# A Fourier transform and two layers on one core: where the row of column D/2 joins z, and where the first two z are made ready

## The chip, the cores and the metric

The kernel runs on one core of a Trainium2 chip, in one launch. The metric is device time in microseconds of that launch. Five engines work side by side: TensorE (PE, with its weight loads as PEld), VectorE (DVE), ScalarE (ACT), GpSimd (POOL) and SyncE (SP), which here does nothing but issue DMAs, one after the other.

## The reference

```
X = fft(fft(x, axis=1), axis=2).real          # x: 8 x 3072 x 256, float32
x1 = X.reshape(24576, 256)
h = x1 @ w_in;  g = h - tanh(h);  x2 = g @ w_out          # 256 -> 2048 -> 256
h2 = x2 @ w_in2                                            # 256 -> 1024
e = exp(h2 - max(h2));  u = h2 * e / (sum(e) + 1e-9)
out = (u - mean(u)) / sqrt(var(u) + 1e-6) * g_ln @ w_out2  # 1024 -> 256
```

## The kernel before

**The transform** (about the first 168 us) goes over 24 pieces q, three for each of 8 batches. For each piece DVE adds and subtracts rows of x (lines 489, 494, 498), PE multiplies by tables (lines 522, 537, 548), and after a batch's third piece ACT copies the sums out of PSUM (lines 586, 592, 600) and they go to DRAM as z: `z1_d[b]` and `z2_d[b]`, each of the form [2, 128, ...]. The partition is a column d from 0 to 127; the first index u says whether column d was added to its mirror column 256 - d or the mirror was subtracted. For d = 0 the difference is not wanted; in its place, row 0 of u = 1, stands the transform of column D/2 = 128, which `transform_nu` makes for all batches together at q = 3 and writes to `n1_d` and `n2_d`. The same stretch also turns the float64 weights into float32 parts (`narrow`, lines 213 to 223).

**The main loop** has 768 steps: 48 groups n of 256 pairs of output rows (6 for each batch), and 16 blocks m of 128 columns of `w_in` in each. A pass is the 16 steps of one group, with j the step in it. In each step PE makes two sums of a block (`parity` and `even`, line 915), DVE mixes them (`lead`, line 933, and `act_in`, line 940), ACT takes the tanh (line 948), DVE subtracts (line 957), ACT rounds and POOL or DVE makes the remainder (lines 178 and 181), and PE multiplies by `w_out` (line 977). In steps with m = 1, 5, 9 and 13 the remainder is DVE's. Pieces of the second layer are laid between by `layer2`: products (line 1006), minimum and exponential (lines 1028, 1047), and the transposition of u through DRAM: DVE transposes 32 x 32 blocks (line 1085), SP stores them to `mv_d` (line 1087) and reads them back in four DMAs to `um` (line 1091).

**How a z comes in.** A group's z passes one buffer `zf` (bufs=1). In the pass before its own, and at the end of the pass ahead of that, it goes so:

- j = 14: `load_z(n + 2)` issues two DMAs from z1_d or z2_d (line 265), when the z before has left the buffer
- j = 0: `load_row(n + 1)` issues one more DMA, of 2.0 to 3.1 KB, from n1_d or n2_d to row 0 of u = 1 of the buffer (line 271)
- j = 2 and j = 10: DVE takes the first and the second sum over it (`mix_z`, lines 287 and 288)
- j = 3: `load_nu(n + 1)` (line 276) brings `nb`, which the next pass uses
- j = 10 and 11: POOL takes two more sums (line 299), ACT rounds to `zs`, POOL makes the remainder

For n = 0 and n = 1 the same is done in the transform at given q, with all four sums and the remainder on DVE; what is put into `later[q]` is woven into the DVE work that stands ahead of piece q, which is that of piece q + 2.

Each engine takes its instructions in the order in which the program lists them, and so does SP with its DMAs: nothing but that order and the waits sets when something runs.

Of the kernel before, what the change touches and what calls it, by code (L numbers as in the profile page):

```python
# [24 lines left out]
NSJ = NS // P  # L25
HP = P // 2
NQB = HP + 2
THIRD = (P, P, P, 2 * NQB, 2 * NQB, 2 * NQB)
# [8 lines left out]
GPB = PAIRS // GP  # L37
# [112 lines left out]
def fft2_moe_moe_kernel(  # L150
    ctx: ExitStack, tc: tile.TileContext, xr, x8, xn, xn8, w_in, w_out, w_in2, w_out2, g_ln, tt, t8, ft, out
):
    nc = tc.nc
# [12 lines left out]
    n1_d = dram.tile([B, 6 * P], F32, name="n1_d")  # L166
    n2_d = dram.tile([B, 2 * ZW], F32, name="n2_d")
    z1_d = [dram.tile([2, P, 6 * P], F32, name=f"z1_d{b}") for b in range(B)]
    z2_d = [dram.tile([2, P, 2 * ZW], F32, name=f"z2_d{b}") for b in range(B)]
# [7 lines left out]
    def rnd(o, i):  # L177
        nc.scalar.activation(out=o, in_=i, func=AF.Copy)  # L178
# [78 lines left out]
    zg, zc = {}, {}  # L257
# [6 lines left out]
        for u in range(2):  # L264
            nc.sync.dma_start(out=zf[:, u, :, :to], in_=src[u].rearrange("p (w n) -> p w n", w=2)[:, :, :to])

    def load_row(n):
        b, g = divmod(n, GPB)
        src = (n1_d if g < NSJ else n2_d)[b : b + 1]
        to = THIRD[g] * (3 if g % 3 else 2)  # L270
        nc.sync.dma_start(out=zc[n][0:1, 1, :, :to], in_=src.rearrange("o (w n) -> o w n", w=2)[:, :, :to])

    def load_nu(n):
        b, g = divmod(n, GPB)
# [28 lines left out]
    def ready_z(n):  # L303
        yield from mix_z(n, nc.vector)
        yield from sums_z(n, nc.vector)
# [250 lines left out]
    def out_tile(name):  # L556
        return hlp.tile([P, 2 * ZW + 2], F32, tag="zt", bufs=5, name=name)
# [23 lines left out]
    def evict(b):  # L581

        for u in range(2):
            zt = out_tile(f"zt{b}_1_{u}")[:, : 6 * P]
            for w, p in enumerate(acc.pop((1, u))):
                nc.scalar.copy(out=zt[:, w * 3 * P : (w + 1) * 3 * P], in_=p[:, : 3 * P])
            nc.sync.dma_start(out=z1_d[b][u], in_=zt)
        for u in range(2):
            zt = out_tile(f"zt{b}_2_{u}")[:, : 2 * ZW]
            if u == 0:  # L590
                for w, p in enumerate(acc[2, u]):
                    nc.scalar.copy(out=z1536[:, 2 * w : 2 * w + 2, b], in_=p[:, NQB : 3 * NQB + 1 : 2 * NQB])
                if b == B - 1:
                    nc.gpsimd.tensor_tensor(
                        out=z1536[:, 4:6], in0=z1536[:, 0:2], in1=z1536[:, 2:4], op=ALU.subtract
                    )
                    for _ in range(2):
                        nc.gpsimd.tensor_tensor(out=z1536[:, 4], in0=z1536[:, 4], in1=z1536[:, 5], op=ALU.add)
            for w, p in enumerate(acc.pop((2, u))):
                nc.scalar.copy(out=zt[:, w * ZW : (w + 1) * ZW], in_=p[:, :ZW])  # L600
            if u == 0 and b == B - 1:
                rnd(zh[:, 0], z1536[:, 4])
                rest(nc.gpsimd, zh[:, 1], z1536[:, 4], zh[:, 0])
            (nc.scalar if b < B - 1 else nc.sync).dma_start(out=z2_d[b][u], in_=zt)
# [117 lines left out]
    def low(o, i, hi):  # L722
        yield rest(nc.vector, o, i, hi)
# [24 lines left out]
    ready, later = [], {}  # L748
    for q in range(NQ):
        b, j = divmod(q, NSJ)  # L750
        ending = now[:]
        now.clear()
        works = []
        if ahead <= q + 2 < NQ:
            works.append(prep(q + 2))
        works += ready + later.pop(q, [])
        weave(*works)
        weave(*ending)
        ready = coming_weights(q + 1)
        if folds and j == 0:  # L760
            later.setdefault(q + 2, []).append(fold_w_in(*folds.pop()))
        if q == 3:
            transform_nu()
        transform(q)
        if j == NSJ - 1 and q < NQ - 1:
            evict(b)
        for n in range(2):
            if q == 13 + 4 * n:
                load_z(n)
                load_nu(n)  # L770
            if q == 14 + 4 * n:
                load_row(n)
                later.setdefault(q + 1, []).append(ready_z(n))
            if q == 15 + 4 * n:
                whole, hi, lo = by_half(n)
                rnd(hi, whole)
                later.setdefault(q + 2, []).append(low(lo, whole, hi))
        if q == NQ - 4:
            nc.sync.dma_start(out=wnu, in_=wnu_d.rearrange("o (m p) -> p (o m)", p=P))
            nc.sync.dma_start(  # L780
                out=nu_h, in_=nu_d[:, PAIRS : PAIRS + 1].rearrange("b o -> o b").to_broadcast([P, B])
            )
# [49 lines left out]
    def split_wi2(eng, b):  # L832
        split_halves(eng, wi2[:, b, 0], wi2[:, b, 1], whole_of(b))
# [9 lines left out]
    def load_wo2(half):  # L843
        w = wk.tile([P, FF2], F32, tag="u", bufs=3, name=f"wo2r_{half}").rearrange("p (k n) -> p k n", k=4)
        nc.sync.dma_start(out=w, in_=wo2_d[half])
        wg.append((w, wk.tile([P, 4, D], F32, tag="ut", bufs=2, name=f"wg{half}")))
# [358 lines left out]
    for step in range(steps + 3):  # L1205
        n, j = divmod(step, NM)
        if step in at_ab:
            special(at_ab[step])
        if 0 < step <= steps:
            parity(*divmod(step - 1, NM), 1)  # L1210
        if step < steps:
            even(n, j)
        if 0 < step <= steps:
            act_in(*divmod(step - 1, NM))
        if step < steps:
            lead(n, j)
        lag = 3 if step < NM else 2
        for s in range(out_done, min(step - lag + 1, steps)):
            act_out(*divmod(s, NM))
        out_done = max(out_done, min(step - lag + 1, steps))  # L1220
        if step - 1 in wo2_at:
            split_wo2(wo2_at.index(step - 1), True)
        layer2(step, "ahead")
        if 1 < n < NG and j == 3:
            sum_x2(S1)
            sum_x2(S2)
        layer2(step, "early")
        if NM <= step < steps + 2:
            low_by_vector(*divmod(step - 2, NM))
        if step in at_o1:  # L1230
            special(at_o1[step])
        if step in (NM - 1, NM):
            mean_wo2(step - NM + 1)
        if step == NM + 2:
            nc.tensor.matmul(bank_b, wi2[:, B11, 0, :P], wi2[:, B11, 0], start=True, stop=True)
        s1 = step - 5 if step < NM else step - 3
        for s in (range(o1_done, min(s1 + 1, steps))):
            o1(*divmod(s, NM))
        o1_done = max(o1_done, min(s1 + 1, steps))
        layer2(step, "late")  # L1240
        if 0 < n < NG and j in (3, 4):
            for b in ((S3,), (S4,))[j - 3] if n > 1 else ((S1, S2), (S3, S4))[j - 3]:
                sum_x2(b)
        if step in wo1_at:
            c, part = divmod(wo1_at.index(step), 2)
            split_wo1(c + 2, wo1_raw[c + 2], slice(part * 2, part * 2 + 2))
        if step == NM:
            raw1.close()
            mv = pool(mv_stack, "mv", 2, side="right")
        if step in wi2_splits:  # L1250
            split_wi2(nc.gpsimd, wi2_splits[step])
        if step in (2, 3):
            load_wo2(step - 2)
        if 7 <= step < NM - 1:
            gain_wo2(step - 7)
        if step in (NM + 1, NM + 2):
            center_wo2(step - NM - 1)
        if step in wo2_at:
            split_wo2(wo2_at.index(step), False)
        if step == NM + 12:  # L1260
            nc.scalar.copy(out=pas, in_=pa)
        if step == NM + 6:
            special_nu()
        if step == NM + 15:
            special_out()
        if n == NG - 1 and j == 9:

            b12 = zp.tile([P, HF], F32, tag="zf", bufs=1, name="b12")
            nc.sync.dma_start(out=b12, in_=b12_d)
        if n == NG - 1 and j == 12:  # L1270
            split_halves(nc.gpsimd, wt[0][:, 0, 0], wt[0][:, 1, 0], b12)
        if step == NM + 30:
            make_identity(nc, ident)
        if n + 2 < NG and j == 14:
            load_z(n + 2)
        if 1 <= n and n + 1 < NG:
            if j == 0:
                load_row(n + 1)
            if j == 3:
                load_nu(n + 1)  # L1280
            if j == 2:
                mixing = mix_z(n + 1, nc.vector)
            if j in (2, 10):
                next(mixing)
            if j == 10:
                weave(sums_z(n + 1, nc.gpsimd))
            if j == 11:
                whole, hi, lo = by_half(n + 1)
                rnd(hi, whole)
                rest(nc.gpsimd, lo, whole, hi)  # L1290
# [159 lines left out]
```

## Time and profile before

| | |
|---|---|
| median of 3 runs | 2876.41 us (2859.62 to 2878.13) |
| profiled execution | 2867.5 us, of which span 2865.7 us |
| mean granted clock of TensorE | 0.979 of full speed |
| busy: PE, DVE, ACT, POOL | 2701.8, 2312.7, 2039.9, 1981.8 us |
| transform, 0 to 168 us | PE busy 144.15 us, DMA share 0.90 |
| main loop, 168 to 2800 us | PE busy 2496.24 of 2632 us, DMA share 0.43 |

A row of the timeline reads: start and duration in microseconds, engine, line, operation, output<-input, shapes, how many were merged, and in brackets how long the engine had been idle before and what ended that. The duration of merged rows runs from the first start to the last end.

### The profile page before, as it was taken

How to read it: one execution, taken by the hardware profiler on the slowest of the kernel's cores; microseconds unless marked ns; L12 is line 12 of the kernel's file. 1: busy time of each engine (PE TensorE's matmuls, PEld its weight loads, DVE VectorE, ACT ScalarE, POOL GpSimd, SP SyncE). 2: the span in 40 equal slices, each digit the busy share in tenths (PEclk: the TensorE clock that was granted, in tenths of full speed). 3: DMA queues.
4: the chain of work that ended last, by engine and by line, in shares of the span. 5: the costliest groups of instructions: out<-in, count | busy, mean ns of one | idle time of the engine just before them, and what ended most of it. 6: DMA issues, size and time to landing. Idle time of an engine off the chain costs nothing.

```text
span 2865.7 us, 48018 instructions
## 1 busy us (share of the span) xinstructions
PE 2701.8 (94%) x15327; PEld 2394.2 (84%) x15327; DVE 2312.7 (81%) x4830; ACT 2039.9 (71%) x3941; POOL 1981.8 (69%) x1806
## 2 busy tenths in 40 slices
PE   9888999999999999999999999999999999999999
PEld 7677888888888888888888888888888888888888
DVE  8766888788887888788777888788887788888886
ACT  4466777777777777777677777777776777777776
POOL 0057777777777777677677777777776777777774
PEclk9989999999999999999999999999999999999999
DMA  9942444444445344444444444444435344444532
GB/s 364 356 126 54 99 112 97 103 94 109 102 96 113 96 99 111 91 106 98 106 95 97 106 99 93 96 111 98 104 86 114 88 104 97 106 105 93 117 87 67
DMA packets 878307, 322.04 MB, mean 112 GB/s; under 512 B 788640, under 2 KB 836320, under 8 KB 874760
## 3 DMA queue, kind: packets, MB, share of 16 engines
q1 hardware_dynamic: 875736, 313.25, 44.6%
q10 hardware_dynamic: 2016, 5.68, 0.5%
q8 instruction: 122, 2.00, 0.3%
q14 instruction: 129, 1.06, 0.1%
q0 software_dynamic: 304, 0.06, 0.0%
HBM read 180.97 MB, written 137.93 MB: 111 GB/s over the span
## 4 chain that ended last, share of the span: by engine, by line
PE 67%; DVE 11%; DMA 9%; SPq 4%; issue 3%; ACT 3%; POOL 2%; DVEq 0%; ACTq 0%; POOLq 0%
PE x2p L977 27%; PE h L915 14%; PE po L1111 9%; PE bank_a L1006 7%; PE bank_b L1006 5%; DMA zf<-n_d 4%; PE po L1118 4%; SPq L1091 4%; DMA mv_d<-tb 3%; DVE h L940 1%; DVE t L957 1%; DVE gh L181 1%; DVE u L1028 1%; DVE h L957 1%; DVE tb L1085 1%
## 5 line engine op out<-in xcount | busy, mean ns | idle before, releaser
L977 PE MATMUL x2p<-gh,wo 128*128 128x512 f32 x4608 | 1155.9, 387 | 3.7 <-POOL gh L181 3.3
L181 POOL TENSOR_TENSOR gh<-t,gh 128x512 fp32r<-128x512 f32 x584 | 892.2, 1528 | 376.2 <-ACT gh L178 184.9
L977 PEld LDWEIGHTS x2p<-gh,wo 128*128 128x128 f32 x4608 | 843.7, 193 | 131.3 <-POOL gh L181 21.1
L915 PEld LDWEIGHTS h<-zs,wt 128*128 128x128 f32 x4572 | 640.6, 193 | 199.3 <-DVE asb L933 82.5
L948 ACT ACTIVATE t<-h 128x512 f32<-128x512 f32 x762 | 453.4, 595 | 484.0 <-DVE h L940 389.2
L915 PE MATMUL h<-zs,wt 128*128 128x256 f32 x4572 | 665.7, 280 | 128.6 <-DVE gh L181 64.1
L940 DVE SCALAR_TENSOR_TENSOR h<-asb,h 128x256 f32<-128x256 f32 x762 | 323.8, 425 | 274.3 <-PE h L915 271.4
L1111 PE MATMUL po<-wo,ut 128*128 128x512 f32 x1528 | 522.0, 383 | 0.0
L181 POOL TENSOR_TENSOR ut<-um,ut 128x512 fp32r<-128x512 f32 x372 | 477.6, 1284 | 17.8 <-ACT ut L178 14.1
L178 ACT ACTIVATE gh<-t 128x512 fp32r<-128x512 f32 x584 | 369.1, 632 | 162.8 <-DVE t L957 159.4
L181 POOL TENSOR_TENSOR xs<-xb,xs 128x256 fp32r<-128x256 f32 (+1 forms) x282 | 234.4, 831 | 277.6 <-ACT xs L178 154.6
L1118 PE MATMUL po<-wo,ut 128*128 128x256 f32 x1528 | 416.5, 273 | 0.0
L957 DVE TENSOR_TENSOR t<-h,t 128x512 f32<-128x512 f32 x578 | 394.6, 683 | 0.0
L933 DVE SCALAR_TENSOR_TENSOR asb<-nb,wnu,h 128x256 f32<-128x256 f32 x762 | 362.3, 475 | 21.5 <-PE h L915 21.4
L1006 PE MATMUL bank_a<-wi,xs 128*128 128x512 f32 x1128 | 319.3, 393 | 2.5 <-ACT bank_b L1154 1.4
L1111 PEld LDWEIGHTS po<-wo,ut 128*128 128x128 f32 x1528 | 290.2, 190 | 30.3
L1056 DVE SCALAR_TENSOR_TENSOR u<-u,e 128x1024 f32<-128x1024 f32 x188 | 300.9, 1600 | 0.0
L1118 PEld LDWEIGHTS po<-wo,ut 128*128 128x128 f32 x1528 | 293.5, 192 | 0.1
L1006 PEld LDWEIGHTS bank_a<-wi,xs 128*128 128x128 f32 x1128 | 213.0, 195 | 39.0 <-ACT bank_b L1154 8.9
L1006 PE MATMUL bank_b<-wi,xs 128*128 128x512 f32 x846 | 229.8, 380 | 1.8 <-POOL xs L181 1.1
L178 ACT ACTIVATE ut<-um 128x512 fp32r<-128x512 f32 x372 | 229.7, 617 | 1.4 <-PE po L1118 0.7
L1085 DVE STREAM_TRANSPOSE tb<-u 128x1024 f32<-128x1024 f32 x186 | 229.4, 1233 | 0.0
(164 smaller groups left out, 3136.6 us busy)
## 6 DMA issues: line engine op xcount, KB each, us to landing
mv_d<-tb SPq DMA_DIRECT2D x186, 512.0 KB, 2.6
um<-mv_d SPq DMA_DIRECT2D x744, 128.0 KB, 3.7
out<-o SPq DMA_DIRECT2D x192, 128.0 KB, 2.0
x<-xr SPq DMA_DIRECT2D x23, 1024.0 KB, 10.8
zf<-z_d SPq DMA_DIRECT2D x32, 396.0 KB, 4.5
zf<-z_d SPq DMA_DIRECT2D x32, 384.0 KB, 4.7
wi<-w_in SPq DMA_DIRECT2D x6, 1024.0 KB, 9.0
z_d<-zt SPq DMA_DIRECT2D x16, 384.0 KB, 8.7
```

The source lines that it names most:

```text
L178: nc.scalar.activation(out=o, in_=i, func=AF.Copy)
L181: eng.tensor_tensor(out=o, in0=i, in1=hi.bitcast(F32), op=ALU.subtract)
L915: nc.tensor.matmul(in_pairs(hs[n, m][:, 0]), wt[c][:, hw, u, o : o + P], in_turn(zs[:, hz, u]), start=(u == 0 and i == 0), stop=(i == 2), ...
L933: nc.vector.scalar_tensor_tensor(out=asb, in0=zg[n][0], scalar=wnu[:, m : m + 1], in1=hs[n, m][:, 0], op0=ALU.mult, op1=ALU.add)
L940: nc.vector.scalar_tensor_tensor(out=h[:, 1], in0=as_.pop((n, m)), scalar=2.0, in1=h[:, 0], op0=ALU.mult, op1=ALU.subtract)
L948: nc.scalar.activation(out=t, in_=h, func=AF.Tanh)
L957: nc.vector.tensor_tensor(out=g, in0=h, in1=t, op=ALU.subtract)
L977: nc.tensor.matmul(in_pairs(x2p[n][mt]), wo1[c][:, hw, k, mt * P : (mt + 1) * P], in_turn(gh[:, hg]), start=(m == 0 and i == 0), stop=(m = ...
L1006: nc.tensor.matmul(in_pairs(bank), xs[:, hx, xs_at[a]], in_turn(wi2[:, b, hw]), start=(start and q == 0), stop=(q == 2), skip_group_check= ...
L1056: nc.vector.scalar_tensor_tensor(out=u, in0=u if h is None else h, scalar=-1.0 if h is None else 1.0, in1=e, op0=ALU.mult, op1=ALU.mult, a ...
L1111: nc.tensor.matmul(in_pairs(po), ut[:, 0, ks], wo2[:, k].rearrange("p h x n -> p (x n) h"), start=(k == 0), stop=False,)
L1118: nc.tensor.matmul(in_pairs(po[:, :D]), ut[:, 1, ks], wo2[:, k, :, 0].rearrange("p h n -> p n h"), start=False, stop=(k == NK2 - 1),)
```

## The change

`load_row` goes, and with it one small DMA into SBUF for each of 48 groups. `put_rows(b)` comes: two DMAs from DRAM to DRAM, which put batch b's rows from n1_d and n2_d to row 0 of u = 1 of z1_d[b] and z2_d[b]. It is called at q = 7, 10, ... 22 for batches 0 to 5 and at steps 8 and 9 of the main loop for batches 6 and 7. The loads of z then bring the row along. For n = 0 the load moves from q = 13 to q = 10, the four sums from 15 to 13, the rounding from 15 to 14, the remainder from 17 to 15; for n = 1 the load from 17 to 16, the rounding from 19 to 20, while the sums stay at 19 and the remainder at 21. (Line numbers behind line 271 are two lower after the change.)

```diff
-    def load_row(n):
-        b, g = divmod(n, GPB)
-        src = (n1_d if g < NSJ else n2_d)[b : b + 1]
-        to = THIRD[g] * (3 if g % 3 else 2)
-        nc.sync.dma_start(out=zc[n][0:1, 1, :, :to], in_=src.rearrange("o (w n) -> o w n", w=2)[:, :, :to])
+    def put_rows(b):
+        for z_d, n_d in ((z1_d, n1_d), (z2_d, n2_d)):
+            nc.sync.dma_start(out=z_d[b][1, 0:1], in_=n_d[b : b + 1])
...
         if j == NSJ - 1 and q < NQ - 1:
             evict(b)
+        if j == 1 and b > 1:
+            put_rows(b - 2)
         for n in range(2):
-            if q == 13 + 4 * n:
+            if q == 10 + 6 * n:
                 load_z(n)
                 load_nu(n)
-            if q == 14 + 4 * n:
-                load_row(n)
-                later.setdefault(q + 1, []).append(ready_z(n))
-            if q == 15 + 4 * n:
+                later.setdefault(q + 3, []).append(ready_z(n))
+            if q == 14 + 6 * n:
                 whole, hi, lo = by_half(n)
                 rnd(hi, whole)
-                later.setdefault(q + 2, []).append(low(lo, whole, hi))
+                later.setdefault(q + 1, []).append(low(lo, whole, hi))
...
         if step in (2, 3):
             load_wo2(step - 2)
+        if step in (8, 9):
+            put_rows(step - 2)
...
         if 1 <= n and n + 1 < NG:
-            if j == 0:
-                load_row(n + 1)
             if j == 3:
                 load_nu(n + 1)
```

SP in the main loop, from the load of one z to the `nb` that follows it, before:

```order
L265 DMA zf_2183<-z_d_77 128x2x264 [waits DMAHW7_49,Pool_49]
L265 DMA zf_2183<-z_d_77 128x2x264
L1087 DMA mv_d_85<-tb_2239 128x1024 [waits DMAHW0_49,DVE_49]
L1091 DMA um_2242<-mv_d_85 32x32x32 [waits DMAHW0_49]
L1091 DMA um_2242<-mv_d_85 32x32x32 [waits DMAHW2_49]
L1091 DMA um_2242<-mv_d_85 32x32x32 [waits DMAHW3_49]
L1091 DMA um_2242<-mv_d_85 32x32x32 [waits DMAHW4_49]
L271 DMA zf_2183<-n_d 1x2x264 [waits DMAHW7_49,DMAHW5_49]
L276 DMA nb_2352<-nu_d 128x256 [waits DMAHW6_49]
```

and with the change:

```order
L265 DMA zf_2196<-z_d_77 128x2x264 [waits DMAHW4_49,DMAHW3_49,Pool_49]
L265 DMA zf_2196<-z_d_77 128x2x264
L1085 DMA mv_d_85<-tb_2252 128x1024 [waits DMAHW5_49,DVE_49]
L1089 DMA um_2255<-mv_d_85 32x32x32 [waits DMAHW5_49]
L1089 DMA um_2255<-mv_d_85 32x32x32 [waits DMAHW7_49]
L1089 DMA um_2255<-mv_d_85 32x32x32 [waits DMAHW0_49]
L1089 DMA um_2255<-mv_d_85 32x32x32 [waits DMAHW1_49]
L274 DMA nb_2364<-nu_d 128x256 [waits DMAHW2_49]
```

The row's DMA behind the four of `um` is gone, and nothing stands in its place. A DMA's first wait is most often that for the semaphore (DMAHW0 to 7, used in turn) that it is to take; Pool and DVE are waits for engines.

DVE in the transform around the four sums of z 0 (zf_841), before, in the work ahead of piece q = 15:

```order
L489 TENSOR_TENSOR sm_2_910<-x_2_770 128x1024 [waits DMAHW5_49]
L287 TENSOR_TENSOR zf_841<-zf_841 128x4x128 [waits DMAHW2_49,DMAHW1_49,DMAHW0_49]
L494 TENSOR_TENSOR pm_2_911<-sm_2_910 128x512 [waits DVE_49,PE_49]
L494 TENSOR_TENSOR pm_2_911<-sm_2_910 128x512
L288 TENSOR_TENSOR zf_841<-zf_841 128x4x128 [waits DVE_49]
```

and with the change the same place, where the remainder of z 0 (zs_715) now stands; its sums are 18 rows further ahead:

```order
L487 TENSOR_TENSOR sm_2_920<-x_2_780 128x1024 [waits DMAHW4_49]
L181 TENSOR_TENSOR zs_715<-zf_710,zs_715 128x512 [waits Activation_49]
L492 TENSOR_TENSOR pm_2_921<-sm_2_920 128x512 [waits DVE_49,PE_49]
L492 TENSOR_TENSOR pm_2_921<-sm_2_920 128x512
L496 TENSOR_TENSOR pm_2_921<-pm_2_921 128x256 [waits DVE_49] x2
```

DVE waits there for ACT instead of DMAs. ACT's rounding of z 0, for which it waits, stands behind the copies of batch 4 now:

```order
L598 COPY zt_2_1_915<-pz_2_1_0_818 128x396 [waits PE_49]
L598 COPY zt_2_1_915<-pz_2_1_1_819 128x396 [waits PE_49]
L602 DMA z_d_81<-zt_2_1_915 128x792 [waits DMAHW4_49,Activation_49]
L178 ACTIVATE zs_715<-zf_710 128x512 [waits DMAHW3_49,DVE_49]
L213 ACTIVATE wo_f<-wo_837 128x1024 [waits DMAHW6_49]
```

Before, five instructions for weights (lines 213, 214 and three of 178) stood between those copies and the rounding of z 0; now it comes right behind them.

## Rows read from the trace of the kernel before

**Rows 1.** Spans and clock: core, span, mean granted clock of TensorE.

```profile
core 0: 2865.7 us, clock 0.979
```

**Rows 2.** Stretches: bounds, length, busy us (count) by engine, granted clock, DMA share, GB/s.

```profile
0.00:168.00 168.00, 144.15 (x898) 117.93 (x899) 131.75 (x209) 70.88 (x129) 5.35 (x15) 0.92 0.90 330
168.00:2800.00 2632.00, 2496.24 (x14066) 2221.17 (x14066) 2136.15 (x4537) 1922.24 (x3716) 1947.28 (x1756) 0.98 0.43 100
928.00:984.00 56.00, 53.65 (x307) 47.59 (x305) 45.69 (x96) 40.75 (x79) 43.31 (x40) 1.00 0.43 103
60.00:104.00 44.00, 43.12 (x267) 33.64 (x265) 43.68 (x58) 24.85 (x46) 1.18 (x2) 1.00 0.99 367
104.00:167.00 63.00, 44.32 (x286) 38.70 (x285) 41.18 (x63) 22.27 (x39) 0.48 (x1) 0.81 0.75 269
```

**Rows 3.** Waits of PE and DVE: us in total, times, longest us.

```profile
PE h L915 <- DVE gh L181: 64.1, 45, 1.8
PE h L915 <- DVE asb L933: 63.8, 47, 4.2
DVE zf L287 <- DMA zf<-n_d: 179.8, 46, 9.4
```

**Rows 4.** Timeline of SP in one pass of the main loop.

```profile
1027.69 1.15 SPq L265 DMA_DIRECT2D zf<-z_d  x2
...
1035.23 2.76 SPq L1091 DMA_DIRECT2D um<-mv_d  x4
1038.09 0.46 SPq L271 DMA_DIRECT2D zf<-n_d  x1
```

**Rows 5.** Timeline of PE, DVE and POOL in the same pass.

```profile
1011.17 0.70 DVE L288 TENSOR_TENSOR zf<-zf 128x528 f32<-128x528 f32 x1
1011.33 1.68 POOL L181 TENSOR_TENSOR gh<-t,gh 128x512 fp32r<-128x512 f32 x1 [1.44 <-ACT gh L178]
...
1036.82 0.74 DVE L1028 CUSTOM_DVE_ANT_0 u<-bank_b,nothing_more,st 128x512 f32<-128x512 f32 x1
1037.65 1.28 POOL L181 TENSOR_TENSOR gh<-t,gh 128x512 fp32r<-128x512 f32 x1 [1.26 <-ACT gh L178]
1038.21 0.83 PE L915 MATMUL h<-zs,wt 128*128 128x256 f32 x6
...
1040.19 1.46 PE L977 MATMUL x2p<-gh,wo 128*128 128x512 f32 x6
1041.13 1.10 DVE L287 TENSOR_TENSOR zf<-zf 128x528 f32<-128x528 f32 x1 [3.56 <-DMA zf<-n_d]
1042.15 0.42 DVE L940 SCALAR_TENSOR_TENSOR h<-asb,h 128x256 f32<-128x256 f32 x1
1042.48 0.47 DVE L933 SCALAR_TENSOR_TENSOR asb<-nb,wnu,h 128x256 f32<-128x256 f32 x1
...
1043.01 0.60 PE L915 MATMUL h<-zs,wt 128*128 128x256 f32 x3 [1.36 <-DVE asb L933]
...
1045.04 0.60 PE L915 MATMUL h<-zs,wt 128*128 128x256 f32 x3 [1.44 <-DVE gh L181]
```

**Rows 6.** Timeline of PE after such a pause in another pass.

```profile
1604.33 2.61 PE L977 MATMUL x2p<-gh,wo 128*128 128x512 f32 x6
```

**Rows 7.** A stretch of 2 us there, columns as in Rows 2.

```profile
1604.00:1606.00 2.00, 2.00 (x7) 1.67 (x7) 1.43 (x4) 1.22 (x4) 1.42 (x2) 0.50 0.00 0
```

**Rows 8.** Timeline of DVE and PE in the transform.

```profile
114.55 0.69 DVE L287 TENSOR_TENSOR zf<-zf 128x512 f32<-128x512 f32 x1 [10.66 <-DMA z_d<-zt]
115.90 3.78 PE L522 MATMUL pz<-tts,pm 64*128 64x128 f32 x32 [4.07 <-DVE pm L494]
145.45 0.69 DVE L287 TENSOR_TENSOR zf<-zf 128x512 f32<-128x512 f32 x1 [9.41 <-DMA zf<-n_d]
150.41 6.46 PE L522 MATMUL pz<-tts,pm 128*128 128x256 f32 x16 [13.77 <-ACT zt L586]
```

**Rows 9.** The DMAs of line 265 (loads of z), us from issue to landing.

```profile
DMA to landing us min/median/max: 3.5/4.5/11.1
```

## The prediction

> **What bounds the kernel now.** I read the stretches first, then the waits, then the timeline of one pass. The stretches [rows 2] show two regimes. In the main loop TensorE is busy 2496 of 2632 us, and between its pauses it is the bound; the reader is to see that no other engine comes near (DVE 2136, POOL 1947, ACT 1922) and that DMA is at 0.43. In the transform it is otherwise: from 60 to 104 us DVE is busy 43.68 of 44 us, the DMA share is 0.99 and PE has 43.12, all three full at once.
>
> The waits [rows 3] then say where PE's 136 idle microseconds of the main loop are. Nearly all stand at line 915 in two groups of about 45, so two a pass: 63.8 us until DVE's line 933, 64.1 us until DVE's line 181, 127.9 together, of which a handful of short ones in the first steps make some 1 us. I take 127, or 2.8 us a pass. DVE in turn waits 46 times at its first sum over z for the row's DMA, 179.8 us in all. One of the 46, 9.41 us, is in the transform [rows 8]; the 45 others make 170.4, or 3.79 each.
>
> The timeline shows the chain. SP issues the load of z at 1027.69, then it is busy with the column moves, whose four DMAs take it from 1035.23 to 1037.99, and only then, at 1038.09, issues the row of a few KB [rows 4]. DVE is done with line 1028 at 1037.56, waits 3.56 us, and starts its sum at 1041.13. Lines 940 and 933 stand behind that sum, so asb is ready at 1042.95 and PE, whose products ended at 1041.65, goes on at 1043.01. It stops again until 1045.04, since the remainder of line 181 is as late [rows 5]. The big load has nothing to do with it: at its median of 4.5 us to landing [rows 9], issued by 1028.84 at the latest, it is there by about 1033.4.
>
> **The change part by part.** *The 46 rows in the main loop.* Each takes an SP issue (0.46 us here [rows 4]) and a wait with it. After the change DVE's first sum waits for the load alone, and that has 8.7 us from the last issue to DVE's arrival at 1037.56. At the longest landing, 11.1 us [rows 9], DVE would wait 2.4 us instead of 3.56; at the median nothing. I take nothing. What is late next? The sum takes 0.70 us where DVE is undisturbed and 1.10 here [rows 5], so it ends between 1038.3 and 1038.7. PE's products for line 940 end at 1039.04 (1038.21 + 0.83), so the sum fits into time in which DVE would wait for PE anyway. From there lines 940 and 933 take 0.8 us (1042.15 to 1042.95): asb is ready near 1039.9, 1.8 us before PE's products run out. The first pause goes entirely. For the second, the way from the start of line 940 to PE's second restart was 2.89 us (1042.15 to 1045.04); started at 1039.1 it ends at 1042.0, and PE gets there at 1041.65 plus some 0.4 for three products. That is just in time, not by much, so I leave 0.2 us a pass, 45 x 0.2 = 9, rounded to 10. Gain 127 - 10 = **117**. Bounds: nothing left (127), or 0.8 a pass left (91).
>
> Against this speaks one thing more. Beside DVE's second sum at 1011.17, 0.70 us long, POOL's line 181 took 1.68 us, and 1.28 in its other row [rows 5], so one of the two pays some 0.4 us; the sum would now start at 1037.56 and POOL's at 1037.65. The Trainium skill, "SBUF — State Buffer", section "Who interferes with whom", says that a DVE instruction with both inputs in SBUF and a GpSimd instruction that reads SBUF exclude each other, the later one blocked to the end of the first. By that rule, with POOL first, the sum would start only at 1038.93 and end at 1039.63, 0.6 us behind PE's products, and the gain would be smaller by up to 27 us; that lies within my bounds, and its worst form is the first rival.
>
> *The clock.* Over the whole span TensorE's granted clock is 0.979 [rows 1], which is short by 0.021 x 2865.7 = 60 us of full speed. The first 168 us, at 0.92 [rows 2], hold 13 of these; 47 are left for the loop. They stand behind pauses: after one, six products of line 977 take 2.61 us [rows 6] instead of 1.46 [rows 5], and there the granted clock is 0.50, that is 1.2 GHz [rows 7]; a pass with its work uncut has 1.00 (the 56 us from 928) [rows 2]. With no pause I expect hardly any fall. Some of the 47 fell on time in which PE paused anyway, so I take three quarters, **36**; bounds 18 (half of that) and 47.
>
> *The transform.* DVE waits twice for a z that is not there: 10.66 us for z 0, 9.41 us for z 1; ACT's next copies hang on that, and PE loses 4.07 and 13.77 us [rows 8]. The loads of z 0 move three pieces ahead and those of z 1 one, and both now have three pieces to the sums; a piece takes about 6.2 us (168 us less the 20 of the two waits, over 24 pieces), so some 18 us stand against a landing of at most 11.1 [rows 9]. Both waits go. How much the end moves is set by what is left to do: from 104 to 167 us DVE works 41.2 us and DMA carries 269 x 63 = 16.9 MB [rows 2], which at the 367 GB/s of the full stretch takes 46 us. So DMA is next, and the transform could end 17 us sooner, 22 if only DVE counted. What is late then may be DVE's remainder: it waits for ACT's rounding, which now stands behind the copies of a batch, and behind DVE's wait stand the sums of a later piece, for which PE waits. No row shows that wait; below it is nothing, and above I take the two PE pauses that DVE's waits made, 4.07 and 13.77 [rows 8], as the nearest, of which the smaller is the nearer, since nothing there hangs on a DMA. I take 2 us of the 17, so **15**. Bounds 5 and 22.
>
> *The 16 added DMAs.* Twelve stand between loads of x. Each costs SP about the row's 0.46 us [rows 4], some 6 us in all, covered as long as SP has waits for DVE to spend them in; without that cover they come off the 17. For their landing I bound with the loads of z, 3.5 to 11.1 us [rows 9]; the load that needs row 0 of batch 0 comes three pieces behind, and the others later still, so nothing waits. The four at steps 8 and 9 stand ahead of the load of z 2, whose first sum comes at step 18, with 3.4 us a step (2632 us over 768) some 34 us on. Nothing.
>
> **Sum.** Against the profiled execution: 2867.5 - 117 - 36 - 15 = 2699.5, so **2700**. The median of the runs shown is 9 us above that execution; I put this to the clock, whose falls come and go, and do not add it.
>
> **The rivals.** *A half of the pause stays* (0.12). The first pause goes, but the remainder of line 181 stays late, be it because POOL and DVE hold each other up where the sum now starts or because the just-in-time above is not. Then 64 us stay, and half of the clock's falls with them: 2867.5 - 63 - 18 - 12 = 2775. For it: the margin of a tenth of a microsecond worked out above. Against it: that chain hangs on line 940, which waited on the sum alone.
>
> *The wait is only handed on* (0.04). The sum waits for the big load nearly as long as for the row, as it would if every load landed as late as the latest. With 2.4 of 3.56 us left [rows 5, 9], a third of the loop's gain comes, and the transform's 15: 2867.5 - 39 - 12 - 15 = 2801. Against it: the load is issued ahead of these moves [rows 4].
>
> *The clock falls under the unbroken load* (0.03, slower). Without pauses PE would work 2460 us at 0.98 and over. If the granted clock then fell to 1.2 GHz for part of it, each us of full-speed work would take two. It decides from 168 us of such work, 6.8% of the loop; at 10% the time would be 2700 + 246 = 2946. Against it: 56 us with 53.65 busy ran at 1.00 [rows 2], and the falls seen follow a pause.
>
> *The added DMAs hold up the loads of x* (0.03). SP waits at each of the six pairs in the transform for a landing of up to 11.1 us [rows 9], 67 us if DVE feels all of it. With half of it the time is 2700 + 33 = 2733, with all 2767; around 2750. For it: the transform is full, and SP takes its DMAs in order. Against it: what a pair writes behind, the copies of its batch, has been out for five pieces.
>
> **How the numbers follow.** The forecast has 0.78. Its own range is from 2867.5 - 127 - 47 - 22 = 2671 to 2867.5 - 91 - 18 - 5 = 2754. The first rival lies around 2775, the last around 2750. The range from 2670 to 2775 then holds most of the forecast, half of the first rival and most of the last: about 0.8. Over 1% (29 us, about what a measurement of this kernel can tell from no change) faster are the forecast and all rivals but the third, 0.97 together, of which I move 0.04 to within 1% for a cause that is not in this list: 0.93, 0.04 and 0.03.
>
> **What would show it.** The wait of DVE for n_d is gone, and its first sum starts without idle time; PE's two groups of waits at line 915 fall from 127.9 us to some 10; the clock of the loop is over 0.99; a pass shrinks by 3.4 us; DVE has no wait over 5 us from 100 us on in the transform, and line 915 starts near 152 instead of 167 us. The prediction is wrong if DVE's first sum waits for z_d instead, if PE waits for another engine two times a pass, or if the clock stays at 0.98.

## The result and the profile after

| | before | after |
|---|---|---|
| median of the runs, us | 2877.27 (2859.62 to 2888.84, 4 runs) | 2667.57 (2664.04 to 2668.86, 4 runs) |
| ratio, 95% interval | | 0.9274 [0.9226, 0.9323] |
| profiled execution, us | 2867.5 | 2668.86 |
| its span, us, and mean clock | 2865.7, 0.979 | 2666.9, 0.996 |

The change makes the kernel 7.3% faster. The forecast was 2700 with a range from 2670 to 2775: the direction is right, and the time lies 2.4 us below the low end. Of the span 198.8 us are gone, and the sum had 168.

First the span with its clock, and from the page the busy time of the engines and the shares of the chain of waits. They answer to [rows 1].

```profile
core 0: 2666.9 us, clock 0.996
PE 2639.8 (99%) x15327; PEld 2366.9 (89%) x15327; DVE 2318.5 (87%) x4830; ACT 2040.5 (77%) x3941; POOL 2005.5 (75%) x1806
```

TensorE is now busy 99% of the whole span, and no other engine is above 87%. Next the waits, which answer to [rows 3]. The first line is the page's for the products of line 913, which was line 915: behind the last bar stands all idle time of PE in front of them, 8.5 us, and what ended it. The second line shows DVE's only wait at its first sum (us in total, times, longest).

```profile
L913 PE MATMUL h<-zs,wt 128*128 128x256 f32 x4572 | 643.4, 276 | 8.5 <-ACT zt L598 6.8 <-DVE asb L931 0.9 <-DVE gh L181 0.9
```

```profile
DVE zf L285 <- DMA zf<-z_d: 3.5, 1, 3.5
```

Of the 63.8 and 64.1 us that PE waited at this line for asb and for DVE's remainder, 0.9 each are left. DVE's 46 waits for n_d are gone, and one wait for a load, in the transform, is all that it has at its first sum.

The timeline of SP in one pass of the main loop shows why; it answers to [rows 4].

```profile
965.67 1.15 SPq L265 DMA_DIRECT2D zf<-z_d  x2
...
973.06 2.75 SPq L1089 DMA_DIRECT2D um<-mv_d  x4
975.85 0.68 SPq L274 DMA_DIRECT2D nb<-nu_d  x1
```

Nothing that DVE's sum needs stands behind the four column moves any more: the load, row included, was issued by 966.82, 8.65 us before the sum. The timeline of PE, DVE and POOL in that pass answers to [rows 5]:

```profile
974.80 0.74 DVE L1026 CUSTOM_DVE_ANT_0 u<-bank_b,nothing_more,st 128x512 f32<-128x512 f32 x1
975.47 0.70 DVE L285 TENSOR_TENSOR zf<-zf 128x528 f32<-128x528 f32 x1
975.63 1.68 POOL L181 TENSOR_TENSOR gh<-t,gh 128x512 fp32r<-128x512 f32 x1 [1.25 <-ACT gh L178]
976.20 0.83 PE L913 MATMUL h<-zs,wt 128*128 128x256 f32 x6
976.73 0.43 DVE L938 SCALAR_TENSOR_TENSOR h<-asb,h 128x256 f32<-128x256 f32 x1 [0.56 <-PE h L913]
...
978.17 1.46 PE L975 MATMUL x2p<-gh,wo 128*128 128x512 f32 x6
978.89 0.69 DVE L181 TENSOR_TENSOR gh<-h,gh 128x512 fp32r<-128x512 f32 x1
979.47 0.83 PE L913 MATMUL h<-zs,wt 128*128 128x256 f32 x6
```

The sum starts right behind line 1026 with no idle time, and afterwards DVE waits for PE (0.56 us at line 938) where PE had waited for DVE. PE's six products at 979.47 are the two groups of three that stood apart at 1043.01 and 1045.04. The second three fall due at 979.47 + 3 x 0.11 = 979.80 (six in an unbroken stream take 0.67 us, shown under the fourth experiment), and the remainder ends at 978.89 + 0.69 = 979.58: in time by 0.2 us.

Two stretches give the loop as a whole. Both run from the first sum over z 3 to that over z 47, 44 passes with the same work; the columns are as in [rows 2]. Before, then after:

```profile
267.26:2721.07 2453.81, 2328.69 (x13110) 2074.40 (x13111) 2006.09 (x4264) 1794.89 (x3475) 1805.26 (x1630) 0.98 0.44 101
```

```profile
253.51:2522.42 2268.91, 2266.67 (x13104) 2044.24 (x13103) 2010.84 (x4266) 1795.96 (x3477) 1828.48 (x1630) 1.00 0.47 109
```

The 44 passes are 184.9 us shorter, 4.20 each. Of these, 122.9 are idle time of PE (2453.81 - 2328.69 = 125.12 against 2.24). The other 62.0 are busy time of PE, for the same number of products within 6. The clock accounts for only part of them. Before, TensorE's clock was at the lower of its two levels (a granted clock of 0.50, 1.2 GHz) for 88.74 us of these passes, and PE was busy for 80.44 of the 88.74; after, it is at the full level throughout. At the full level that work would take half as long, so the clock's part is about 40.2 us, an estimate from these figures. Where the other 21.8 come from, 0.50 a pass, is what the experiments had to settle.

In the transform, first the row of the kernel before at which the main loop's products begin, then the rows with the change, DVE and PE, that answer to [rows 8], and the stretch from 104 us on:

```profile
167.73 0.60 PE L915 MATMUL h<-zs,wt 128*128 128x256 f32 x3 [0.56 <-ACT zt L600]
```

```profile
132.11 0.69 DVE L285 TENSOR_TENSOR zf<-zf 128x512 f32<-128x512 f32 x1 [3.48 <-DMA zf<-z_d]
154.34 1.01 PE L913 MATMUL h<-zs,wt 128*128 128x256 f32 x3 [6.76 <-ACT zt L598]
```

```profile
104.00:154.00 50.00, 41.43 (x299) 36.50 (x297) 42.68 (x62) 22.48 (x42) 0.55 (x2) 0.98 0.94 354
```

The main loop's first product comes at 154.34 instead of 167.73, 13.4 us sooner. DVE's two waits of 10.66 and 9.41 us shrank to one of 3.48. From 104 us to the end of the transform the DMA share is 0.94 where it had been 0.75 in the 63 us of [rows 2].

### The profile page after: what moved, and what is told of

It reads as the page before. It is cut to its first block, busy times and chain, and to the rows that moved or that the text cites. A ratio compares the mean times of both kernels' runs of the same rounds, so it can differ in the third digit from the quotient of the medians.

```text
span 2666.9 us, 47939 instructions
## 1 busy us (share of the span) xinstructions
PE 2639.8 (99%) x15327; PEld 2366.9 (89%) x15327; DVE 2318.5 (87%) x4830; ACT 2040.5 (77%) x3941; POOL 2005.5 (75%) x1806
## 4 chain that ended last, share of the span: by engine, by line
PE 93%; DVE 3%; DMA 2%; POOL 1%; issue 1%; ACT 1%; SPq 0%; POOLq 0%; DVEq 0%; ACTq 0%
PE x2p L975 36%; PE h L913 19%; PE po L1109 12%; PE bank_a L1004 9%; PE bank_b L1004 7%; PE po L1116 6%; PE pz L520 1%; PE pz L535 1%; DMA wo_d<-wo_f 0%; DMA x<-x 0%; DMA x<-xr 0%; PE pw L437 0%; PE ph L1324 0%; DVE t L955 0%; DVE asb L931 0%
## 5 line engine op out<-in xcount | busy, mean ns | idle before, releaser
L181 POOL TENSOR_TENSOR gh<-t,gh 128x512 fp32r<-128x512 f32 x584 | 923.9, 1582 | 342.8 <-ACT gh L178 162.3
L975 PE MATMUL x2p<-gh,wo 128*128 128x512 f32 x4608 | 1133.9, 381 | 1.8 <-POOL gh L181 1.5
L975 PEld LDWEIGHTS x2p<-gh,wo 128*128 128x128 f32 x4608 | 830.8, 190 | 125.0 <-POOL gh L181 18.7
L913 PE MATMUL h<-zs,wt 128*128 128x256 f32 x4572 | 643.4, 276 | 8.5 <-ACT zt L598 6.8
L1054 DVE SCALAR_TENSOR_TENSOR u<-u,e 128x1024 f32<-128x1024 f32 x188 | 313.7, 1669 | 0.0
L1004 PE MATMUL bank_a<-wi,xs 128*128 128x512 f32 x1128 | 310.0, 383 | 2.5 <-ACT bank_b L1152 1.4
L1004 PEld LDWEIGHTS bank_a<-wi,xs 128*128 128x128 f32 x1128 | 205.9, 189 | 35.7 <-ACT bank_b L1152 8.9
```

What stands on the lines that cost most here:

```text
L181: eng.tensor_tensor(out=o, in0=i, in1=hi.bitcast(F32), op=ALU.subtract)
L913: nc.tensor.matmul(in_pairs(hs[n, m][:, 0]), wt[c][:, hw, u, o : o + P], in_turn(zs[:, hz, u]), start=(u == 0 and i == 0), stop=(i == 2), ...
L975: nc.tensor.matmul(in_pairs(x2p[n][mt]), wo1[c][:, hw, k, mt * P : (mt + 1) * P], in_turn(gh[:, hg]), start=(m == 0 and i == 0), stop=(m = ...
L1004: nc.tensor.matmul(in_pairs(bank), xs[:, hx, xs_at[a]], in_turn(wi2[:, b, hw]), start=(start and q == 0), stop=(q == 2), skip_group_check= ...
L1054: nc.vector.scalar_tensor_tensor(out=u, in0=u if h is None else h, scalar=-1.0 if h is None else 1.0, in1=e, op0=ALU.mult, op1=ALU.mult, a ...
```

## The experiments

The theory of the pauses (Theory A in what was expected) says: the 30 us that the sum missed lie in the main loop, because a pause costs PE more than the idle time that the trace shows. The rival puts them into the transform and the places of the first two z. The line numbers of the changed kernel's loop are 8 higher in the first of these kernels, 6 in the next four, and the same in the last.

**The loop's part alone.** The kernel before, with the rows put into z's tensors and no row loaded in the main loop; z 0 and z 1 keep their places and their rows.

```diff
+    def put_rows(b): ...
+        if j == 1 and b > 1:
+            put_rows(b - 2)
+        if step in (8, 9):
+            put_rows(step - 2)
-            if j == 0:
-                load_row(n + 1)
```

> The rows are put into z's tensors and the 46 row DMAs of the main loop are gone, but the first two z are made ready where the kernel before does it, with their own row DMAs. Theory A (the sum's loop term was too small, since a pause costs more than PE's idle time: drain and restart of its stream, about 0.54 us a pass, beside idle 2.8 and clock 0.85): loop gain about 185 us, a time of 2681 (2668 + the transform's 13), passes of 51.41 us. Rival C (the loop gave the 153 forecast and the transform, or what it hands on, gave the rest): about 2715, passes of about 52.2.

Measured: 2681.83 us (2680.2 to 2684.36, 4 runs), ratio 0.9335 [0.9299, 0.9371]. The span with its clock, and a stretch of its main loop:

```profile
core 0: 2682.6 us, clock 0.994
```

```profile
300.00:2500.00 2200.00, 2196.50 (x12695) 1980.00 (x12694) 1944.90 (x4124) 1739.94 (x3368) 1774.06 (x1579) 1.00 0.47 109
```

PE is idle 3.5 of 2200 us at full clock: the rows' way alone empties the loop of pauses. The transform keeps its waits (DVE waits 11.4 and 10.0 us for z 0 and z 1), and the loop's products begin here:

```profile
168.68 0.60 PE L921 MATMUL h<-zs,wt 128*128 128x256 f32 x3 [0.56 <-ACT zt L604]
```

That is 14.3 us behind the changed kernel's 154.34, and the whole change is 14.3 us faster than this kernel. The theory's number is met.

**The first two z alone.** The changed kernel, with the row's load put back into the main loop where it was; the added DMAs stay.

```diff
+    def load_row(n): ...
+            if j == 0:
+                load_row(n + 1)
```

> All of the change, but the row DMA of the main loop is issued again at j = 0 as before (it writes the same row once more). Theory A: only the transform's gain of 13 us is left, about 2864, with line 915's two pauses a pass and the clock near 0.98. Rival C: the transform's change is worth 45 us, about 2832.

Measured: 2851.29 us (2837.34 to 2857.57, 7 runs), ratio 0.9918 [0.9886, 0.995], or by the ratio 24 us sooner [14, 33]. The span, its waits, and the start of the loop's products:

```profile
core 0: 2855.8 us, clock 0.981
```

```profile
DVE zf L291 <- DMA zf<-n_d: 165.7, 45, 5.1
PE h L919 <- DVE gh L181: 64.5, 45, 1.8
PE h L919 <- DVE asb L937: 61.0, 47, 3.4
```

```profile
155.78 1.01 PE L919 MATMUL h<-zs,wt 128*128 128x256 f32 x3 [7.06 <-ACT zt L604]
```

The loop's three waits are back as they were in [rows 3], less the one of the transform. The loop starts 12.0 us sooner than in the kernel before, so the transform itself is worth no 45 us. The time lies between the two expectations; the 13.4 us of the transform are just below the interval's low end. The seven runs had a mean clock of 0.982, the ten of the kernel before beside them 0.978, and 0.004 x 2850 = 11 us is about what is left; why the clock fell less often is not shown. By the time alone this run does not decide: single executions spread over 20 us, as their clock (0.980 to 0.987) does.

**The row's load kept, but earlier on SP.** The changed kernel with 46 row loads in the loop, now issued behind the load of their z and ahead of the column moves.

```diff
+        if n + 2 < NG and j == 15:
+            load_row(n + 2)
```

> The row DMA of the main loop is there for each z, but issued at j = 15 of the pass ahead, on the same queue and ahead of the column moves of j = 0, not behind them. If the place in SP's order is the cause of the pause: the row lands before DVE comes to its first sum, 2668 to 2690 us. If any small DMA behind the load costs its landing (that is, the number of DMAs counts): 2830 to 2870.

Measured: 2665.43 us, one run; span 2663.6 us at 0.996. SP, then DVE, in one pass:

```profile
962.38 1.21 SPq L265 DMA_DIRECT2D zf<-z_d  x2
967.41 0.24 SPq L271 DMA_DIRECT2D zf<-n_d  x1
970.87 3.89 SPq L1095 DMA_DIRECT2D um<-mv_d  x4
```

```profile
972.18 0.71 DVE L291 TENSOR_TENSOR zf<-zf 128x528 f32<-128x528 f32 x1
```

```profile
DVE zf L291 <- DMA zf<-z_d: 3.3, 1, 3.3
```

The row's DMA is there in every pass, and DVE doesn't wait: the last line is its only wait at this sum, and it is z 1's, in the transform. So neither the DMA nor its size cost the loop its time, but its place behind the column moves in SP's order. By this run, moving that one call brings the loop's whole gain.

**A pause in every second pass.** The changed kernel with the row's load back at its old place for even n only.

```diff
+            if j == 0 and n % 2 == 0:
+                load_row(n + 1)
```

> The row DMA at j = 0 only for every second z, 23 times. Theory A: 23 passes of about 51.9 + 2.8 us and, behind some of them alone, a fall of the clock; the passes between at 51.41 us; 2668 + 23 x 4.2 = 2765. A pass with a pause and no fall of the clock shows 51.95 beside the idle time. Rival B (no fixed price of a pause; the further gain was all clock): such passes show 51.41 beside the idle time. If the clock fell by itself and not behind pauses, it would fall in passes without one too.

Measured: 2768.28 us, one run, clock 0.987. Here passes with and without pauses stand side by side in one execution. A stretch of two passes, one with the two pauses, and the same two passes of the changed kernel:

```profile
420.22:526.33 106.11, 103.35 (x598) 92.87 (x597) 91.20 (x191) 81.58 (x160) 82.91 (x74) 1.00 0.46 108
```

```profile
408.27:511.08 102.81, 102.81 (x598) 92.88 (x597) 90.66 (x189) 81.63 (x160) 83.20 (x74) 1.00 0.49 111
```

Both hold 598 products at a granted clock of 1.00, with no fall in either. The pauses cost 3.30 us, of which 2.76 are idle time and **0.54 are busy time** of PE. The timeline of PE in that pass shows where it is:

```profile
472.35 0.83 PE L919 MATMUL h<-zs,wt 128*128 128x256 f32 x6
473.02 0.38 PE L1115 MATMUL po<-wo,ut 128*128 128x512 f32 x1
...
474.33 1.46 PE L981 MATMUL x2p<-gh,wo 128*128 128x512 f32 x6
477.12 0.60 PE L919 MATMUL h<-zs,wt 128*128 128x256 f32 x3 [1.32 <-DVE asb L937]
479.15 0.60 PE L919 MATMUL h<-zs,wt 128*128 128x256 f32 x3 [1.43 <-DVE gh L181]
479.59 1.46 PE L981 MATMUL x2p<-gh,wo 128*128 128x512 f32 x6
```

In an unbroken stream the next product starts before the row of the last group has ended: six of line 919 start at 472.35 and the next group at 473.02, 0.67 us on, though the row says 0.83; and six of x2p are followed after 979.47 - 978.17 = 1.30 us (the pass of the changed kernel above), though the row says 1.46. Ahead of a pause the full 1.46 counts as busy: 0.16 more. The three at 477.12 count 0.60 where 3 x 0.11 = 0.33 would have passed: 0.27 more. The three at 479.15 are followed after 0.44: 0.11 more. Together 0.54. By these rows it is the end and the new start of a broken stream, which overlap with other products as long as it isn't broken. The ends of products are modelled in the trace, so the parting into idle and busy time is the profile's; the 3.30 us are a difference of lengths and don't depend on it.

**The row twice.** The changed kernel with the row loaded twice at the old place, which lengthens DVE's wait.

```diff
+            if j == 0:
+                load_row(n + 1)
+                load_row(n + 1)
```

> The row DMA at j = 0 twice in a row, so that the second waits for the first on SP and the pause gets some 3 us longer. Theory A (a fixed price for each break of PE's stream): idle of about 5.8 us a pass and still 51.95 beside it in passes without a fall of the clock; more of the passes have a fall; about 2864 + 45 x 3 + 40 = 3040. Rival B2 (the price grows with the pause, as if PE were slower for a time after it): about 52.5 beside the idle time.

Measured: 2961.35 us, one run, against 2860.64 for the kernel before beside it. Span and waits:

```profile
core 0: 2959.2 us, clock 0.957
```

```profile
DVE zf L291 <- DMA zf<-n_d: 237.5, 45, 7.4
PE h L919 <- DVE asb L937: 125.6, 47, 5.9
PE h L919 <- DVE gh L181: 56.5, 45, 1.4
```

The number was missed: a second row made DVE's wait longer by (237.5 - 165.7) / 45 = 1.6 us, about half of what I had put down. But it tells something else. Against the trace of the second experiment, with one row, the span is 103 us longer (2959.2 against 2855.8), and the 44 passes from the first sum over z 3 to that over z 47 are 106.6 longer (2557.56 against 2450.92). Of these, 50.9 are idle time of PE. The clock has the rest: it is 0.957 instead of 0.981, PE was busy at the lower level for 191.08 us instead of 72.83, and half of the difference is 59.1. In this kernel PE's busy time in a pass was at least 53.5 us in all passes but the first, where the changed kernel has 51.41 in most. Whether the 0.54 us grow with the pause can't be read from one pass, since none of these is without a fall of the clock. Over all 44, PE's busy time is 115.5 us above the changed kernel's (2382.15 against 2266.67); without 95.5 for the clock, half of the 191.08, some 20 are left, 0.45 a pass. By this estimate the price does not grow with the pause.

**Less work for SP at the end of the transform.** The changed kernel with ten of the twelve row DMAs of the transform moved into the main loop (the four of steps 8 and 9 move too, within it), and z 1's load one piece earlier, to remove DVE's last wait; beside it the changed kernel again.

```diff
-        if j == 1 and b > 1:
-            put_rows(b - 2)
+        if q == 7:
+            put_rows(0)
-            if q == 10 + 6 * n:
+            if q == 10 + 5 * n:
-                later.setdefault(q + 3, []).append(ready_z(n))
+                later.setdefault(q + 3 + n, []).append(ready_z(n))
-        if step in (8, 9):
-            put_rows(step - 2)
+        if 15 <= step < 22:
+            put_rows(step - 14)
```

> The change, with 14 of the 16 row DMAs moved from the transform into the first pass of the main loop, and the load of z 1 issued one piece sooner (q = 15; its sums stay at 19). If the transform's end hangs on DVE's 3.5 us wait for z 1 and on SP's time between the loads of x: main loop 2 to 6 us sooner, 2662 to 2666 against 2667.6 with the change. If DMA's bytes set the end, they are the same: 2667 to 2669.

> The changed kernel as it is, on the same chip as the run beside it: 2664 to 2669 us by all theories.

Measured: 2666.75 us (2665.72 to 2670.86, 4 runs), ratio 0.9288 [0.9264, 0.9312]; the changed kernel beside it 2668.84 us (2667.42 to 2670.5, 5 runs), ratio 0.9292 [0.9269, 0.9316]. No difference. The transform's end in the trace:

```profile
104.00:154.00 50.00, 45.17 (x308) 38.45 (x307) 44.20 (x65) 23.77 (x45) 0.48 (x1) 1.00 0.99 379
```

```profile
155.91 1.01 PE L913 MATMUL h<-zs,wt 128*128 128x256 f32 x3 [5.72 <-ACT zt L598]
```

DVE's wait for z 1 is gone and the engines do more in the 50 us, but the DMA share is 0.99, and line 913 starts at 155.91 instead of 154.34. So neither z 1's wait nor the added DMAs set the end. At such a share DMA's bytes are the likely bound, but no run here moves fewer of them, so that is not shown. Another order of ACT's work is untested as well: in both traces the chain of waits goes through ACT's conversion of weights (line 214), which waits for a DMA and behind which the last copies of z stand. No kernel that I ran clearly beats the changed one.

## Why the prediction was right, and where not

**The chain of the pauses: right.** Load early, row late behind the column moves, DVE's sum, asb, PE: without the row each link let go as the sum said. The first sum of the pass shown starts at 975.47 without a wait, in all 46 groups of the main loop it has none, it lasts 0.68 to 0.71 us in all but the first of them, and PE's 127.9 us of waits at that line are 1.8. The third experiment shows that SP's order was the cause.

**The 46 rows in the main loop: this step failed, by its size.** Gain 117, predicted from PE's idle time alone; measured about 145, 122.9 of idle time and 22 of busy time. The idle time gave 6 more than the sum since the second pause, for which I kept 10 us "just in time", went too: the remainder comes 0.2 us ahead of its products, and that suffices. The larger part is the price that I did not have: besides its idle time, each pass with two pauses took more of PE's busy time, 0.54 us in the pass of the fourth experiment. Over the 44 passes that would be 44 x 0.54 = 24 us; what the clock leaves of the 62.0 is **22 us**, 0.50 a pass. I read an idle row as the whole cost of a pause; the end of the products before it and the start of those behind it were in the busy time, where they look like work. A row of the kernel before shows it: three products of line 915 have 0.60 us [rows 5] where six in a row have 0.83, and half of that is not 0.60. The bounds of the step, 91 to 127, were made of idle time at both ends; that is why the range's low end came out too high.

**The clock: right.** Predicted 36, against the 40.2 estimated above from PE's busy time at the lower level. The granted clock of the whole span went from 0.979 to 0.996 and stands at 1.00 in the loop. In the loop, falls follow pauses. Of the 44 passes of the fourth experiment, 10 of the 22 with pauses have one, and none of the 22 between them; here is one with a fall, and the pass behind it, each from one first sum to the next:

```profile
367.83:420.22 52.39, 49.52 (x276) 44.18 (x276) 44.79 (x95) 39.31 (x77) 36.91 (x34) 0.97 0.39 92
420.22:475.14 54.92, 54.92 (x321) 49.65 (x320) 45.43 (x96) 42.38 (x83) 44.94 (x41) 1.00 0.52 115
```

In the fifth, with the longest pauses, every pass but the first has a fall.

**The transform: right in size, in part by luck.** Predicted 15, measured 13.4. The wait for which I took 2 us off, DVE's for ACT's rounding, did not come; instead 3.48 us for z 1's load stayed, where the working had both waits gone. It counted three pieces from the load's place in the program; SP was late there:

```profile
119.06 5.48 SPq L265 DMA_DIRECT2D zf<-z_d  x2
```

The two issues took 5.48 us, where they take 1.15 in the loop, since SP waited 4.3 us for an earlier load of x to land, and the sum over z 1 came at 132.11. That DMA is what comes next was in the working; the last experiment agrees with it, but leaves it open.

**The added DMAs: right, nothing.** Their landing in the trace of the changed kernel:

```profile
DMA to landing us min/median/max: 4.1/5.5/6.8
```

That is within the bounds of 3.5 to 11.1 that I took from z's loads, and no load waited for them. The first experiment bounds their cost in the transform: with them alone, the loop began at 168.68 instead of 167.73, 0.95 us later.

**Together.** The span lost 122.9 + 22 + 40 in the loop's 44 passes and 13.4 in the transform, 198.3 of 198.8. Against the sum that is 22 for the breaks, 6 of idle time and 4 of clock more, and 1.6 less in the transform: the 30.6 us between 2699.5 and 2668.86 but for rounding and the first and last passes. Between the medians 209.7 us went, since the median before lies 9.8 us above the profiled execution that the sum started from.

**The rivals.** Half of the pause staying, the wait handed on to the big load, a clock that falls under unbroken load, and added DMAs that hold up x: none came. (The sums of the first two took 12 us for the transform, where the step has 15.) For the third, 2269 us with 2267 of PE's work ran at 1.00.

On POOL and DVE at the port: beside the sum, POOL's line 181 took 1.68 us at 975.63, where it had 1.28 at 1037.65 [rows 5], and over the whole kernel this line went from 892.2 to 923.9 us, 54 ns more for each of 584. In the first group of the main loop it was the other way round:

```profile
204.58 1.56 DVE L285 TENSOR_TENSOR zf<-zf 128x512 f32<-128x512 f32 x1
```

There POOL's line 181 had started at 204.33 and kept 1.27 us. The Trainium skill, "SBUF — State Buffer", section "Who interferes with whom", says that a DVE instruction with two SBUF inputs contends with a GpSimd instruction that reads SBUF, and that the one issued first has its way. The trace agrees: the sum at 975.47 came first, kept its 0.70 us, and POOL paid the 0.4; at 204.58 the sum came second and paid 0.86. The loss of up to 27 us that the prediction bounded needed POOL to come first in every group, and by the sum's length it did so in one of 46.

## What to carry to other kernels

A pause on the engine that bounds the kernel costs its idle time, plus the end and the new start of its stream, plus what the clock loses behind it: here 122.9, 22 and 40 us. Compare a pass with pauses and a pass without them in length, not in idle time, and set the price of a pause by the start of the next product in an unbroken stream. And before a small transfer is taken out, look where it stands in its queue: here, in the one run that tried it, moving it ahead of four slow issues was worth as much as removing it.

## What was not expected of the hardware

- The rows of products overlap in a stream and do not at a break: 0.54 us of busy time for the two breaks of a pass, at a granted clock of 1.00.
- A second small DMA behind the first lengthened DVE's wait by 1.6 us a pass, though the first alone made it wait 3.68 us: the two overlap, so a wait for DMAs in one queue is not their number times one.
- Pauses that were 51 us longer in sum over 44 passes cost 107 us of time, since the granted clock went from 0.981 to 0.957 over the span.
